# The first expert's left halves gathered straight from x2, weight loads that wait for their buffers alone, and another share of the lo parts on VectorE

## The chip, the core and the metric

One core of a Trainium2 chip runs the whole program in one launch. The metric is the device time of an execution in microseconds (us); lower is better. The profile names the engines PE (TensorE, matmuls; PEld is its loading of weights), DVE (VectorE), ACT (ScalarE), POOL (GpSimd) and SP (SyncE, which issues most DMAs).

## The reference, cut to what matters

Three stages follow each other: attention, a product of matrices for each token, and eight experts that choose their tokens greedily.

```python
attn = softmax(pool2(q) @ k.T / 8) @ v           # 4 x 8 heads, 576 pooled rows, head size 64
x    = attn as [2304, 512]                       # 2304 tokens
x2   = ((x @ w1) * (x @ w2)) @ w3 @ w_out        # w1, w2: 512 x 1024; w3: 1024 x 1024; w_out: 1024 x 512
logits = x2 @ w_gate                             # 2304 x 8
for idx in argsort(-logits.flatten()):           # best pair (token, expert) first
    tok, e = idx // 8, idx % 8
    if assigned[tok] < 0 and counts[e] < 288:
        assigned[tok] = e; counts[e] += 1
for e in range(8):                               # 288 tokens each
    out[mask] = relu(x2[mask] @ e1[e]) @ e2[e]   # 512 -> 1024 -> 512
```

All is in float32. An expert can be computed as soon as its 288 tokens are known, and an expert is full once its last token is found; so the lists come one after the other.

## The kernel before

Every matmul of the later stages multiplies float32 numbers that are split into a high and a low part of a shorter format, in three terms: high x high, low x high and high x low. A high part is a copy made by ACT (`x2h`, `uh`, `exh`, `ehh`); the low part is the number minus its high part, made by DVE or POOL (`x2l`, `ul`, `exl`, `ehl`).

After attention (to about 510 us) and the two products that give h (to about 770 us), three stages follow on PE:

- W = w3 @ w_out, from weights that SP loads back (`w<-w3t`) as buffers come free.
- x2 = h @ W, 18 tiles t of 128 tokens, each 24 matmuls of 512 columns in `pb`. The last three tiles (LATE) are done in two halves of 256 columns, all left halves ahead of the right ones. ACT copies the result to `x2o`, and SP stores it to DRAM: the rows in x2 (shown as `x` in the profile), and the left half of every row once more in x2a.
- the experts, in the order in which their lists come. An expert's rows are gathered by POOL through indirect DMAs (`g<-x,idx`), transposed on PE (`ident,g`), split into `exh` and `exl`, and multiplied: 96 matmuls of 128x288 with the first weights (`exh/exl` with `uh/ul`) and 96 with the second (`ehh/ehl` with `uh/ul`). Eight experts are 1,536 matmuls. The results are transposed back and scattered by POOL.

Only the first expert has its gather in two: the left halves from x2a with its list `idx` into `early`, and the right halves from x2 read as half rows, with `idx_right` = 2 idx + 1. Left halves are there earlier than right ones, so its first six accumulations (AHEAD) begin with the left half of the rows.

Beside W, x2 and the experts a search runs for the next full expert, in seven phases of about 40 to 54 us. It is a loop of round trips: DVE makes masks (`rt_mask`), PE counts with them (`rt_oh,rt_mask`), DVE works on the counts (`rt_cnt`, `rt_own`), PE sums again (`rt_own,rc_ones`), and so on. A phase ends when DVE makes `rt_rows`; from it follow the expert's number (`rows`, which SP reads into a register by a TENSOR_LOAD to address that expert's weights), and its list: `sl_rows`, `sl_oh`, 18 matmuls `sl_mv,sl_oh`, then `idx`.

An expert's weights come in eight pieces ("units") of 128x1024, loaded by SP into a ring of three raw buffers (`u`), whose high part ACT makes and whose low part POOL makes for the first six experts (n < BESIDE = 6), POOL or DVE for the last two. Thirteen such units have room; the first four are kept as halves of 512 columns. Units beyond the fourth wait in three ways: for a raw buffer, for the end of x2 (`gate_main`), and, from HELD = 4 on, for the gathers of the first expert to be issued.

The order of each engine is fixed before the program runs, by a list scheduler that knows a cost for each operation and takes, at each engine, the waiting operation with the lowest priority number. Engines execute strictly in that order. Lines L1501 to L1530 store x2, L1555 to L1586 load and split the units, L1619 ff. gather, L1655 ff. compute an expert.

Of the kernel before, what the change touches and what calls it, by code (L numbers as in the profile page):

```python
# [11 lines left out]
F32 = mybir.dt.float32  # L12
# [1156 lines left out]
def moe_and_experts(tc, sch, env, w1, w2, w3, w_out, w_gate, e1, e2, out):  # L1169
# [330 lines left out]
    def x2_part(t, h, n, xs, xo, pr):  # L1500

        (xh, kxh), (xl, kxl) = xs
        xo, kxo = xo
        cols = slice(h * n, h * n + n)
        ps = Hold(sB)
        for k in range(KF):
            for i, (a, b) in enumerate(((xh, Wh), (xh, Wl), (xl, Wh))):
                def fn(a=a, b=b, k=k, i=i):
                    nc.tensor.matmul(ps.tile[:, :n], a[:, k, :], b[:, k, cols], start=(k == 0 and i == 0), stop=(k == KF - 1 and i == 2))
                acc_op("PE", c_mm(n), fn, [(kxh, k // 4), (kxl, k // 4)] + whole * (t > 1) + [("Wh", k), ("Wl", k)], ps, k == i == 0, pr)  # L1510
        sch.op("ACT", c_act(n), lambda: evac("ACT", xo[:, cols], ps.tile[:, :n]), uses=[ps], w=[(kxo, h)], prio=pr)
        (b, s_), (b1, s1) = divmod(2 * t, NS), divmod(2 * t + 1, NS)

        for dst, w, width, key in ((x2a, DM // 2, DM // 2, "x2a"), (x2, DM, n, "x2")):
            if key == "x2a" and h:
                continue

            for rows, at in ((slice(0, 64), b * SP + s_), (slice(64, 128), b1 * SP + s1)):
                def fn(dst=dst, w=w, width=width, rows=rows, at=at):
                    nc.sync.dma_start(dram(dst, at * w + h * n, [[NS * w, 64], [1, width]]), xo[rows, h * n:h * n + width])  # L1520
                sch.op("DMA", 500, fn, r=[(kxo, h)], w=[(key, t, h)], prio=pr, lat=2300)

    def x2_split(t, pr, lo_e):
# [33 lines left out]
    def unit(w, n, k, pr):  # L1557
# [3 lines left out]
        count[0] += 1  # L1561
        sch.gate = [] if first else gate_main
        raw, free = tt.next([128, 1024], F32, f"u{c}", ("ur", c))
        o = sch.op("DMA", 600, lambda: nc.sync.dma_start(raw[:, :], w[bass.ds(first_row[n][0] + 128 * k, 128), :]), r=[("row", n)],
                   w=[("ur", c)] + free, prio=pr, lat=2800)
        tt.first(o)
        unit_loads.append(o)
        halves = (0, 1) if i < n_pre else (None,)

        lo_e = ("DVE", "POOL") if n >= BESIDE else ("POOL",)  # L1570
        if us[i] is None:
# [45 lines left out]
    def gather(e, pr):  # L1617
# [11 lines left out]
        for h in range(2 if e == 0 else 1):  # L1629
            for j in range(3):  # L1630
                if e == 0:
                    (i2, ki2), keys = (idx2, "idx2") if h else (idx[0], ("idx", 0)), [gs[h][j][1]]
                    dst, src = gs[h][j][0], x2[:, :].rearrange("n (h d) -> (n h) d", h=2) if h else x2a[:, :]
                else:
                    i2, ki2, keys, dst, src = idx[e], ("idx", e), [gs[x][j][1] for x in range(2)], lambda g=rows[j]: g, x2[:, :]

                def fn(j=j, i2=i2, dst=dst, src=src):
                    nc.gpsimd.indirect_dma_start(out=dst(), out_offset=None, in_=src,
                                                 in_offset=bass.IndirectOffsetOnAxis(ap=i2[:, j:j + 1], axis=0))
                sch.gate = [] if e == 0 and h == 0 else gate_main  # L1640
                gathers.append(sch.op("POOL", 1000, fn, r=[ki2] + (x2rows[0] if e == h == 0 else x2rows[1]), w=keys, prio=pr, lat=2500))
        sch.gate = gate_main
# [122 lines left out]
def attention_moe_experts_kernel(ctx, tc, q, k, v, w1, w2, w3, w_out, w_gate, e1, e2, out):  # L1765
# [10 lines left out]
    for r in regions.values():  # L1776
# [40 lines left out]
```

## Time and profile before

| | us |
|---|---|
| median of 3 runs (lowest, highest) | 1228.44 (1225.3, 1230.96) |
| profiled execution, its own time | 1225.08 |
| its span | 1223.3 |
| PE busy / PEld / DVE / ACT / POOL | 1161.6 / 1095.7 / 971.8 / 655.9 / 658.9 |

The span is the time between the first and the last instruction of the profiled execution; its own time is a little longer. The profile numbers each expression by its line; nearly all work of the later stages goes through one helper and has L113, so rows are told apart by their tiles. In a row `out<-in` names what is written and read, and a number in brackets is the time the engine sat idle before it and what ended that. PEclk is the TensorE clock that was granted, 1.00 being full speed.

### The profile page before, as it was taken

The page shows a single profiled execution, that of the slowest core. Times are in us where ns is not written, and L with a number is a line of the kernel's source. Part 1 is how long each engine was busy: PE and PEld are TensorE (multiplying, and loading weights), DVE is VectorE, ACT ScalarE, POOL GpSimd, SP SyncE. Part 2 cuts the span into 40 slices and gives each one's busy share as a digit, 9 for nine tenths or more (in the row PEclk, how much of TensorE's full clock was granted, in tenths as well). Part 3 has the DMA queues.
Part 4 walks back from the last instruction along what each step waited for, and adds up shares of the span by engine and source line. Part 5 has one row for each costly group of instructions (what it writes and reads, how often), then busy time and mean ns, then how long its engine had stood idle before and what let it go on. Part 6 is the DMA issues. An engine that isn't in the chain of part 4 may idle for free.

```text
span 1223.3 us, 24304 instructions
## 1 busy us (share of the span) xinstructions
PE 1161.6 (95%) x8377; PEld 1095.7 (90%) x8377; DVE 971.8 (79%) x2902; ACT 655.9 (54%) x1365; POOL 658.9 (54%) x672
## 2 busy tenths in 40 slices
PE   6999999999999999999999999999998979889996
PEld 5999999999999999889999999777768969889996
DVE  7998999999999999997877787676677687785541
ACT  6887888888888888542222220223222445345530
POOL 4565666666666655554333244236444777679320
PEclk9999999999999999999999999999998989899998
DMA  9676666666666653135555533443224444446620
GB/s 212 153 167 153 152 152 152 152 152 152 151 150 153 151 114 93 41 106 179 168 189 179 173 104 104 145 157 76 59 64 125 158 165 153 142 150 209 201 78 23
DMA packets 116619, 169.89 MB, mean 139 GB/s; under 512 B 47959, under 2 KB 79710, under 8 KB 116494
## 3 DMA queue, kind: packets, MB, share of 16 engines
q1 hardware_dynamic: 113326, 158.89, 48.3%
q0 software_dynamic: 3168, 9.44, 2.5%
q8 instruction: 66, 1.08, 0.4%
q14 instruction: 59, 0.48, 0.1%
HBM read 104.87 MB, written 24.45 MB: 106 GB/s over the span
## 4 chain that ended last, share of the span: by engine, by line
PE 78%; DVE 15%; issue 2%; POOL 1%; DMA 1%; ACT 1%; SPq 0%; DVEq 0%; POOLq 0%; ACTq 0%
PE pb L113 37%; PE s L590 12%; PE pt L614 7%; PE pt L113 6%; PE pt L664 6%; PE s L664 5%; DVE pt L113 4%; PE s L614 3%; DVE cv_v L113 2%; DVE sl_oh L113 1%; PE pt L543 1%; DVE p L600 1%; DVE idx L113 1%; DMA z<-y 1%; DMA vr<-in_v_dram 1%
## 5 line engine op out<-in xcount | busy, mean ns | idle before, releaser
L600 DVE TENSOR_SCALAR_CACHE_REDUCE p<-s 128x384 f32<-128x384 f32 x432 | 230.2, 551 | 34.0 <-PE pt L614 12.5
L590 PE MATMUL s<-kst,qst 128*128 128x384 f32 x768 | 199.7, 359 | 6.3 <-DVE p L600 4.0
L605 ACT ACTIVATE p<-p,mn 128x1152 f32<-128x1152 f32 x144 | 181.1, 1258 | 23.6 <-DVE mn L603 21.4
L113 PE MATMUL pb<-xhi,wh 128*128 128x288 f32 x512 | 156.8, 306 | 1.7 <-ACT wh L113 1.7
L113 PE MATMUL pb<-xlo,wh 128*128 128x288 f32 x512 | 152.5, 298 | 1.9 <-DVE xlo L113 1.7
L113 PE MATMUL pb<-xhi,wl 128*128 128x288 f32 x512 | 152.2, 297 | 1.1 <-DVE wl L113 1.1
L113 POOL TENSOR_TENSOR ul<-u,uh 128x512 fp32r<-128x512 f32 (+1 forms) x68 | 123.9, 1844 | 40.3 <-ACT uh L113 40.0
L590 PEld LDWEIGHTS s<-kst,qst 128*128 128x128 f32 x768 | 123.2, 190 | 12.6 <-DVE p L600 8.8
L614 PE MATMUL pt<-ident,p 128*128 128x128 f32 x879 | 132.8, 273 | 0.3 <-ACT p L605 0.3
L648 DVE TENSOR_TENSOR p_lo<-pt,p_hi 128x384 fp32r<-128x384 f32 x230 | 124.6, 551 | 0.6 <-ACT p_hi L331 0.6
L331 ACT ACTIVATE p_hi<-pt 128x384 fp32r<-128x384 f32 x230 | 106.6, 492 | 12.1 <-PE pt L614 11.7
L614 PEld LDWEIGHTS pt<-ident,p 128*128 128x128 f32 x879 | 107.4, 141 | 4.4 <-ACT p L605 0.5
L113 DVE SCALAR_TENSOR_TENSOR cv_v<-cv_raw,cv_v 128x512 int32<-128x512 int32 (+1 forms) x120 | 102.2, 856 | 6.6 <-POOL cv_raw L113 4.4
L113 PEld LDWEIGHTS pb<-xlo,wh 128*128 128x128 f32 x512 | 97.5, 190 | 2.7 <-DVE xlo L113 2.7
L113 PEld LDWEIGHTS pb<-xhi,wh 128*128 128x128 f32 x512 | 97.4, 190 | 2.5 <-ACT wh L113 1.9
L113 PEld LDWEIGHTS pb<-xhi,wl 128*128 128x128 f32 x512 | 97.3, 190 | 1.3 <-DVE wl L113 1.3
L341 POOL TENSOR_TENSOR p_lo<-praw,p_hi 128x384 fp32r<-128x384 f32 x96 | 97.0, 1018 | 0.4
L113 ACT ACTIVATE a<-pb 128x288 f32<-128x288 f32 x64 | 26.3, 411 | 132.2 <-PE pb L113 126.0
L335 POOL CAST p_hi<-praw 128x384 fp32r<-128x384 f32 x96 | 47.6, 506 | 82.2 <-ACT praw L331 82.1
L113 POOL TENSOR_TENSOR cv_raw<-cv_raw 128x512 f32<-128x512 f32 x40 | 43.2, 1080 | 86.5 <-DVE cv_v L113 67.3
L113 PE MATMUL pb<-ehh,uh 128*128 128x288 f32 x256 | 80.1, 313 | 0.0
L113 PE MATMUL pb<-exh,uh 128*128 128x288 f32 x248 | 78.9, 318 | 0.1
(315 smaller groups left out, 3285.5 us busy)
## 6 DMA issues: line engine op xcount, KB each, us to landing
u<-in_moe_w_dram SPq DMA_DIRECT2D x64, 512.0 KB
cv_raw<-in_moe_w_dram SPq DMA_DIRECT2D x32, 512.0 KB
vr<-in_v_dram SPq DMA_DIRECT2D x32, 288.0 KB
kr<-in_k_dram SPq DMA_DIRECT2D x32, 288.0 KB
kst<-kH SPq DMA_DIRECT2D x31, 288.0 KB
kst<-kL SPq DMA_DIRECT2D x31, 288.0 KB
qr<-in_q_dram SPq DMA_DIRECT2D x15, 576.0 KB
w3t<-wg SPq DMA_DIRECT2D x16, 512.0 KB
```

What stands on the lines that cost most here:

```text
L113: return f(*[x.get() if isinstance(x, Lazy) else x for x in a], **{n: x.get() if isinstance(x, Lazy) else x for n, x in k.items()})
L331: nc.scalar.activation(out, in_, AF.Copy)
L335: nc.gpsimd.tensor_copy(out, in_)
L341: (nc.vector if eng == "DVE" else nc.gpsimd).tensor_tensor(out, a, b, op=OP.subtract)
L543: nc.tensor.transpose(ps.tile[:, a * 128:(a + 1) * 128], r[:, 3 * c + a, :, :].rearrange("p h d -> p (h d)"), ident)
L590: nc.tensor.matmul(ps.tile[:, :384], a[:, :], b[:, cs], start=(n == 0), stop=(n == len(passes) - 1))
L600: sch.op("DVE", c_dve(384), lambda ps=ps, c=c, cs=cs: nc.vector.tensor_scalar(t[:, cs], ps.tile[:, :384], 1.0, BIG, op0=OP.mult, op1=OP.mi ...
L605: sch.op("ACT", c_act(S, psum=False, acc=True), lambda: nc.scalar.activation(t, t, AF.Exp, bias=mn[:, 3:4], scale=-1.0, accum_out=sm[0][:, ...
L614: nc.tensor.transpose(ps.tile[:, a * 128:(a + 1) * 128], t[:, b * 128:(b + 1) * 128], ident)
L648: sch.op("DVE", c_dve(384), lambda view=view, src=src: nc.vector.tensor_tensor(view(lo), src(), view(hi).bitcast(F32), op=OP.subtract), us ...
L664: nc.tensor.matmul(ps.tile[:, :n], vt[:, t, :, :], src[half][:, t, off:off + n], start=(half == 0 and t == 0), stop=(half == 1 and t == NT ...
```

## The change

Three things change.

- x2a and its 36 stores are gone. The first expert's left halves are gathered from x2 read as half rows, with a new list `idx_left` = 2 idx, one more DVE operation. As left gathers and stores of right halves now touch the same array, they are declared independent (`apart`). Six stores from `L16` (64x256) into the right halves of the last three tiles' rows are put at the start of the W stage; the real ones overwrite them.
- A unit's load waits for its raw buffer alone: not for the end of x2, nor for gathers. Its splits still wait as before.
- Low parts of the units of the experts 1, 2, 7 and 8 (n < FILLED = 2 or n >= 6) are made by DVE, those of the experts 3 to 6 by POOL.

```diff
@@ -1491,7 +1491,13 @@
-    x2, x2a = env["x2"], env["x2a"]
+    x2 = env["x2"]
+    halves = {"gathers": [], "stores": []}
+
+    def apart(kind, o):
+        for p in halves["stores" if kind == "gathers" else "gathers"]:
+            tc.declare_no_dep(o.ins, p.ins, reason="the other halves of rows")
+        halves[kind].append(o)
...
@@ -1511,14 +1517,13 @@
-        for dst, w, width, key in ((x2a, DM // 2, DM // 2, "x2a"), (x2, DM, n, "x2")):
-            if key == "x2a" and h:
-                continue
-
-            for rows, at in ((slice(0, 64), b * SP + s_), (slice(64, 128), b1 * SP + s1)):
-                def fn(dst=dst, w=w, width=width, rows=rows, at=at):
-                    nc.sync.dma_start(dram(dst, at * w + h * n, [[NS * w, 64], [1, width]]), xo[rows, h * n:h * n + width])
-                sch.op("DMA", 500, fn, r=[(kxo, h)], w=[(key, t, h)], prio=pr, lat=2300)
+
+        for rows, at in ((slice(0, 64), b * SP + s_), (slice(64, 128), b1 * SP + s1)):
+            def fn(rows=rows, at=at):
+                o = nc.sync.dma_start(dram(x2, at * DM + h * n, [[NS * DM, 64], [1, n]]), xo[rows, h * n:h * n + n])
+                if h:
+                    apart("stores", o)
+            sch.op("DMA", 600, fn, r=[(kxo, h)], w=[("x2", t, h)], prio=pr, lat=2300)
@@ -1530,6 +1535,12 @@
+    for t in range(LAST, N // 128):
+        for x in range(2):
+            b, s_ = divmod(2 * t + x, NS)
+            sch.op("DMA", 600, lambda b=b, s_=s_: nc.sync.dma_start(dram(x2, (b * SP + s_) * DM + DM // 2, [[NS * DM, 64], [1, DM // 2]]),
+                   L16[0:64].rearrange("p c e -> p (c e)")[:, 0:DM // 2]), r=["L16"], w=[("x2", t, 1)], prio=P_W, lat=2300)
@@ -1559,15 +1570,15 @@
-        sch.gate = [] if first else gate_main
+        sch.gate = []
...
         tt.first(o)
-        unit_loads.append(o)
+        sch.gate = [] if first else gate_main
         halves = (0, 1) if i < n_pre else (None,)
-        lo_e = ("DVE", "POOL") if n >= BESIDE else ("POOL",)
+        lo_e = ("POOL",) if FILLED <= n < BESIDE else ("DVE",)
@@ -1594,9 +1605,9 @@
-    x2rows = [[("x2a", t, 0) for t in range(N // 128)], [("x2", t, h) for t in range(N // 128) for h in range(1 + (t >= LAST))]]
+    x2rows = [[("x2", t, 0) for t in range(N // 128)], [("x2", t, h) for t in range(N // 128) for h in range(1 + (t >= LAST))]]
@@ -1629,16 +1640,18 @@
-                    (i2, ki2), keys = (idx2, "idx2") if h else (idx[0], ("idx", 0)), [gs[h][j][1]]
-                    dst, src = gs[h][j][0], x2[:, :].rearrange("n (h d) -> (n h) d", h=2) if h else x2a[:, :]
+                    (i2, ki2), keys = ((idx2, "idx2"), (idx1, "idx1"))[1 - h], [gs[h][j][1]]
+                    dst, src = gs[h][j][0], x2[:, :].rearrange("n (h d) -> (n h) d", h=2)
...
+                    if e == h == 0:
+                        apart("gathers", o)
@@ -1719,14 +1732,14 @@
+    idx1 = rreg.tile([96, 3], I32, name="idx_left")
...
+    sch.op("DVE", 70, lambda: nc.vector.tensor_scalar(idx1, idx[0], 2.0, None, op0=OP.mult), r=[("idx", 0)], w=["idx1"], prio=P_L)
...
-    for o in unit_loads[HELD:]:
-        o.sdeps.update(gathers)
@@ -1754,7 +1767,7 @@
-HELD = 4
+FILLED = 2
```

The scheduler then orders all engines anew. Three places show it. `x_216` in the rows on SP is x2, and numbers behind a name tell its copies apart.

On PE, at the end of x2 and the start of the first expert, before (the list's matmuls `sl_mv,sl_oh`, then the transposes of the left halves, `early`):

```order
L113 LDWEIGHTS sl_oh_9626
L113 MATMUL pt_67<-sl_mv_10056,sl_oh_9626 96x6
L113 MATMUL pt_65<-ident,early 128x96 x3
L113 MATMUL pt_66<-ident,early 128x96 x3
L113 LDWEIGHTS rt_mask_9273
L113 MATMUL pt_67<-rt_oh_9230,rt_mask_9273 90x48
...
L113 MATMUL pb_6498<-exh_10952,uh_0_9669 128x288
L113 MATMUL pb_6498<-exl_10958,uh_0_9669 128x288
L113 MATMUL pb_6498<-exh_10952,ul_0_9689 128x288
```

On PE at the same place in the changed kernel, from the last routing matmuls beside x2 on (`rc_ones` and `rc_tris` are constants):

```order
L113 LDWEIGHTS rt_mask_9215
L113 MATMUL pt_65<-rt_oh_9232,rt_mask_9215 90x48
L113 LDWEIGHTS rc_ones_145
L113 MATMUL pt_67<-rt_own_9188,rc_ones_145 128x120
L113 LDWEIGHTS rc_tris
L113 MATMUL pt_66<-sl_rows_10046,rc_tris 128x1
L113 MATMUL pt_65<-ident,early 128x96 x3
L113 MATMUL pt_67<-ident,early 128x96 x3
L113 MATMUL pb_6497<-exh_10905,uh_0_9674 128x288
L113 MATMUL pb_6497<-exl_10908,uh_0_9674 128x288
L113 MATMUL pb_6497<-exh_10905,ul_0_9680 128x288
```

The transposes of the left halves now stand directly behind the matmul of `sl_rows`, and the first expert's matmuls ahead of the list's; before they stood behind the list.

On DVE, in the fourth phase of the search, beside the first expert, before:

```order
L113 TENSOR_TENSOR rt_mask_9273<-pt_68,rt_thr_9269 128x270
L113 TENSOR_TENSOR exl_10958<-pt_66,exh_10952 128x288 x2
L113 TENSOR_TENSOR rt_cnt_9286<-pt_66,rc_diag 90x48
L113 TENSOR_REDUCE pt_68<-rt_cnt_9286 90x8
L113 TENSOR_TENSOR rt_own_9188<-pt_68,rc_thr 90x120
L113 SCALAR_TENSOR_TENSOR ehl_11097<-pb_6498,ehh_11089 128x288
L113 SCALAR_TENSOR_TENSOR ehl_11106<-pb_6526,ehh_11095 128x288
L113 SCALAR_TENSOR_TENSOR ehl_11116<-pb_6520,ehh_11102 128x288
L113 TENSOR_REDUCE pt_68<-pt_66 128x15
L113 SCALAR_TENSOR_TENSOR ehl_11124<-pb_6478,ehh_11114 128x288
```

On DVE at the same place in the changed kernel (`u` and `uh` are a unit's raw buffer and its high part):

```order
L113 TENSOR_TENSOR rt_mask_9215<-pt_68,rt_thr_9312 128x270
L113 TENSOR_TENSOR ul_11019<-u_10970,uh_11007 128x1024
L113 TENSOR_TENSOR exl_10908<-pt_65,exh_10905 128x288
L113 TENSOR_TENSOR ul_11028<-u_10987,uh_11021 128x1024
L113 TENSOR_TENSOR ul_11041<-u_11003,uh_11026 128x1024
L113 TENSOR_TENSOR exl_10908<-pt_65,exh_10905 128x288
L113 TENSOR_TENSOR rt_cnt_9245<-pt_65,rc_diag 90x48
L113 TENSOR_REDUCE pt_68<-rt_cnt_9245 90x8
L113 TENSOR_TENSOR rt_own_9188<-pt_68,rc_thr 90x120
L113 TENSOR_TENSOR ul_11084<-u_11024,uh_11068 128x1024
L113 TENSOR_REDUCE pt_68<-pt_65 128x15
L113 SCALAR_TENSOR_TENSOR ehl_11104<-pb_6497,ehh_11082 128x288
```

Low parts of units (`ul`, 1024 columns) now stand between the steps of the search. In the whole phase there are nine of 1024 and six of 512 columns; before there were none.

On SP, at the end of x2's stores, before (`rows` is the third expert's number, `u` the load of the next unit):

```order
L113 DMA x_216<-x2o_9803 64x256
L113 DMA x2a<-x2o_9865 64x256
L113 DMA x_216<-x2o_9865 64x256 x2
L113 DMA x_216<-x2o_9803 64x256
L1606 TENSOR_LOAD rows_10866
L113 DMA x_216<-x2o_9865 64x256
L113 DMA x_216<-x2o_9739 64x256 x2
L113 ISA
L113 DMA u_10997<-in_moe_w_dram 128x1024
```

On SP at the same place in the changed kernel:

```order
L113 DMA x_216<-x2o_9861 64x256
L113 DMA x_216<-x2o_9806 64x256
L113 DMA x_216<-x2o_9744 64x256
L113 DMA x_216<-x2o_9861 64x256
L1617 TENSOR_LOAD rows_10860
L113 DMA x_216<-x2o_9744 64x256
L113 ISA
L113 DMA u_10970<-in_moe_w_dram 128x1024
```

The last store now stands behind the load of the number, where three did before, and no store to x2a is left.

Counted in the order of PE, this many of the experts' 1,536 matmuls stand ahead of these points:

| point in the search | before | now |
|---|---|---|
| matmuls of the third list | 0 | 18 |
| rows that end phase 4 | 192 | 267 |
| rows that end phase 5 | 453 | 543 |
| rows that end phase 6 | 720 | 786 |
| the last list | 807 | 897 |

On DVE eight low parts of 512 columns stand in the first phase, where there were none. In the fourth phase there are now 8 exl and 13 ehl instead of 3 and 8, and the two `x2l` that stood in it come ahead of it; in the fifth there are 19 exl and ehl instead of 20, in the sixth 12 instead of 16. On POOL the fourth phase has 4 low parts of 1024 and 2 of 512 columns instead of 9 and 3.

## Rows read from the trace of the kernel before

**Rows 1.** The page's chain that ended last, by engine.

```profile
PE 78%; DVE 15%; issue 2%; POOL 1%; DMA 1%; ACT 1%; SPq 0%; DVEq 0%; POOLq 0%; ACTq 0%
```

**Rows 2.** Windows: length, busy us (count) of PE, PEld, DVE, ACT, POOL; PEclk, DMA, GB/s.

```profile
809.10:849.70 40.60, 38.35 (x202) 28.80 (x202) 30.16 (x122) 14.24 (x25) 24.27 (x23) 1.00 0.37 104
849.70:889.80 40.10, 38.11 (x202) 28.69 (x202) 29.10 (x121) 10.51 (x19) 17.66 (x17) 1.00 0.28 64
889.80:930.20 40.40, 37.89 (x242) 30.92 (x242) 29.66 (x122) 10.42 (x19) 16.21 (x16) 1.00 0.26 60
930.20:980.00 49.80, 43.54 (x326) 41.03 (x324) 34.58 (x135) 18.13 (x32) 32.91 (x23) 0.90 0.50 157
980.00:1034.00 54.00, 46.73 (x357) 45.08 (x357) 41.40 (x141) 26.82 (x50) 41.10 (x37) 0.91 0.48 160
1034.00:1084.40 50.40, 44.75 (x348) 43.17 (x347) 39.09 (x137) 20.68 (x39) 37.79 (x32) 0.93 0.48 158
1084.40:1105.50 21.10, 17.16 (x155) 16.64 (x155) 19.32 (x66) 10.02 (x21) 14.45 (x21) 1.00 0.40 130
1105.50:1213.50 108.00, 105.45 (x811) 104.72 (x810) 47.97 (x70) 43.15 (x82) 42.33 (x40) 1.00 0.42 133
```

**Rows 3.** TensorE's longest waits, 939 to 1106: total us, times, longest.

```profile
PE pt L113 <- DVE exl L113: 8.4, 4, 2.8
PE pt L113 <- DVE rt_mask L113: 4.0, 2, 3.6
```

**Rows 4.** TensorE's groups, 1105.5 to 1213.5: count, busy, mean, idle before.

```profile
L113 PE MATMUL pb<-ehh,uh 128*128 128x288 f32 x128 | 38.3, 299 | 0.0
L113 PE MATMUL pb<-exl,uh 128*128 128x288 f32 x115 | 34.0, 296 | 0.0
```

**Rows 5.** Timeline of VectorE: start, duration, operation, idle before.

```profile
1142.53 0.69 DVE L113 TENSOR_TENSOR ul<-u,uh 128x512 fp32r<-128x512 f32 x1 [1.38 <-ACT uh L113]
1162.43 1.23 DVE L113 TENSOR_TENSOR ul<-u,uh 128x1024 fp32r<-128x1024 f32 x1 [1.00 <-ACT uh L113]
```

**Rows 6.** Timeline of SyncE, GpSimd and TensorE, 929 to 945.

```profile
929.41 1.09 SPq L113 DMA_DIRECT2D x2a<-x2o  x2
...
932.90 0.59 SPq L113 DMA_DIRECT2D x2a<-x2o  x1
933.53 7.32 SPq L113 DMA_DIRECT2D x<-x2o  x6
935.95 1.61 POOL L113 DMA_INDIRECT early<-x2a,idx  x1 [2.54 <-DMA x<-x2o]
941.91 1.38 PE L113 MATMUL pt<-sl_mv,sl_oh 128*96 128x6 bf16 x12 [2.50 <-DVE sl_oh L113]
943.30 0.95 POOL L113 DMA_INDIRECT g<-x,idx_right  x1 [1.97 <-DMA x<-x2o]
```

**Rows 7.** Timeline of SyncE, loads of the W stage.

```profile
773.65 25.06 SPq L113 DMA_DIRECT2D w<-w3t  x9
```

**Rows 8.** VectorE's and GpSimd's groups by form, 820 to 1213.

```profile
L113 DVE SCALAR_TENSOR_TENSOR ehl<-pb,ehh 128x288 fp32r<-128x288 f32 x62 | 27.5, 451 | 17.9 <-ACT ehh L113 14.1 <-issue 2.6 <-ACT uh L113 0.7
L113 DVE TENSOR_TENSOR x2l<-hraw,x2h 128x512 fp32r<-128x512 f32 x2 | 1.4, 684 | 0.0
L113 POOL TENSOR_TENSOR ul<-u,uh 128x1024 fp32r<-128x1024 f32 x34 | 80.9, 2399 | 33.4 <-ACT uh L113 33.1
```

**Rows 9.** VectorE's waits, 930.2 to 980.

```profile
DVE rt_cnt L113 <- PE pt L113: 4.4, 5, 1.4
DVE pt L113 <- PE pt L113: 3.8, 4, 1.0
```

**Rows 10.** Timeline of VectorE and GpSimd around two idx operations.

```profile
944.58 0.17 DVE L113 SCALAR_TENSOR_TENSOR idx<-sl_fl 96x3 int32<-96x3 f32 x1
1047.77 7.31 POOL L113 TENSOR_TENSOR ul<-u,uh 128x512 fp32r<-128x512 f32 x5
1051.27 3.84 DVE L113 SCALAR_TENSOR_TENSOR idx<-sl_fl 96x3 int32<-96x3 f32 x1
```

More of the change, by code (lines that the diff above doesn't have):

```diff
@@ L1596, in moe_and_experts @@
     r_y, r_o = ring(P3, "ey", 4, [128, CAP], F32), ring(P3, "eo", 3, [96, DM], F32)
-    scat, unit_loads, gathers = [], [], []
+    scat = []
     spacer = G.tile([1, 1], F32, name="spacer")
-    x2rows = [[("x2a", t, 0) for t in range(N // 128)], [("x2", t, h) for t in range(N // 128) for h in range(1 + (t >= LAST))]]
+    x2rows = [[("x2", t, 0) for t in range(N // 128)], [("x2", t, h) for t in range(N // 128) for h in range(1 + (t >= LAST))]]
     first_row = [[] for _ in range(8)]
@@ L1631, in gather, with fn @@
                 if e == 0:
-                    (i2, ki2), keys = (idx2, "idx2") if h else (idx[0], ("idx", 0)), [gs[h][j][1]]
-                    dst, src = gs[h][j][0], x2[:, :].rearrange("n (h d) -> (n h) d", h=2) if h else x2a[:, :]
+                    (i2, ki2), keys = ((idx2, "idx2"), (idx1, "idx1"))[1 - h], [gs[h][j][1]]
+                    dst, src = gs[h][j][0], x2[:, :].rearrange("n (h d) -> (n h) d", h=2)
                 else:
                     i2, ki2, keys, dst, src = idx[e], ("idx", e), [gs[x][j][1] for x in range(2)], lambda g=rows[j]: g, x2[:, :]
-                def fn(j=j, i2=i2, dst=dst, src=src):
-                    nc.gpsimd.indirect_dma_start(out=dst(), out_offset=None, in_=src,
-                                                 in_offset=bass.IndirectOffsetOnAxis(ap=i2[:, j:j + 1], axis=0))
+                def fn(j=j, h=h, i2=i2, dst=dst, src=src):
+                    o = nc.gpsimd.indirect_dma_start(out=dst(), out_offset=None, in_=src,
+                                                     in_offset=bass.IndirectOffsetOnAxis(ap=i2[:, j:j + 1], axis=0))
+                    if e == h == 0:
+                        apart("gathers", o)
                 sch.gate = [] if e == 0 and h == 0 else gate_main
-                gathers.append(sch.op("POOL", 1000, fn, r=[ki2] + (x2rows[0] if e == h == 0 else x2rows[1]), w=keys, prio=pr, lat=2500))
+                sch.op("POOL", 1000, fn, r=[ki2] + (x2rows[0] if e == h == 0 else x2rows[1]), w=keys, prio=pr, lat=2500)
         sch.gate = gate_main
@@ L1786, in attention_moe_experts_kernel @@
     env = {"nc": nc, "G": G, "xT": xT, "main": regions["main"], "prep": regions["prep"], "psS": regions["psS"],
-           "s_pt": s_pt, "pts": pts, "ident": ident, "rc": rc, "xreg": regions["x"], "x2": dpool.tile([N, DM], F32, name="x2"), "x2a": dpool.tile([N, DM // 2], F32, name="x2a"), "w3t": dpool.tile([8, 128, 2, 1024], F32, name="w3t"),
+           "s_pt": s_pt, "pts": pts, "ident": ident, "rc": rc, "xreg": regions["x"], "x2": dpool.tile([N, DM], F32, name="x2"), "w3t": dpool.tile([8, 128, 2, 1024], F32, name="w3t"),
            "wof": dpool.tile([8, 128, 2, DM], F32, name="wof")}
```

## The prediction

> **What bounds the kernel now.** The chain that ended last is three quarters TensorE [rows 1], so I cut the part after the W stage into stretches at the points where routing has found its rows, the mark where one expert's search ends and the next begins [rows 2]. In the first three stretches (beside x2) TensorE is busy for 38 of 40 us and VectorE for 29 to 30, so TensorE sets the pace and VectorE has about 10 us free in each. In the next three TensorE is busy for 43.54 of 49.80, 46.73 of 54.00 and 44.75 of 50.40 us, and in the fourth, up to the last list's matmuls, for 17.16 of 21.10: 6.26 + 7.27 + 5.65 + 3.94 = 23.1 us without work, and its granted clock in the first three is 0.90 to 0.93 of full. The waits behind that name VectorE, above all the exl parts and the routing masks [rows 3]. In the last stretch TensorE is busy for 105.45 of 108.00 us: nothing but its own work bounds it.
>
> So the end is the time at which the last list is known, plus the expert matmuls that still stand behind it on TensorE. After the last list 729 of the 1,536 (3 x 128 + 3 x 115) run in 108.0 us [rows 2, 4]: 108.0 / 729 = 0.148 us each, transposes included. A change helps by making the last list earlier or by putting matmuls ahead of it. This one does the second at the price of the first: counted in TensorE's order, 897 expert matmuls stand before the last list instead of 807, so 639 stay behind it, 90 fewer.
>
> **The change, part by part**, as shifts of the end.
>
> *Matmuls behind the last list.* 90 x 0.148 = -13.3 us. This holds only if TensorE does them in time it now loses, since its whole work is unchanged: they must fit into the 23.1 us above.
>
> *The search of phases 1 to 3 gets later.* Eight lo parts of 512 columns go from GpSimd to VectorE in phase 1: 8 x 0.69 = 5.5 us by the one at 1142.53 [rows 5]. VectorE has about 10 us free in that stretch, but in pieces between round trips, and the parts stand in its order where the search stands too. TensorE's order says the same: the routing rows that end phase 1 come after the equivalent of 126 x2 matmuls of 512 columns instead of 112, those that end phase 3 after 420.5 instead of 403.5. In a stretch of 40.1 to 40.4 us some 146 of these pass, 0.275 us each with all that lies between, so 14 are 3.9 us and 17 are 4.7. I take +4; the bounds are 0 (all eight in the gaps) and +5.5 (none). x2 itself does not end later, as TensorE has other work in its order meanwhile.
>
> *Left halves gathered from x2.* The 36 stores into the copy cost SP about 0.55 us each to issue (two in 1.09 us), and the last of them, at 932.90, stands behind x2's own stores; the first early gather goes out at 935.95 [rows 6]. With the left halves stored once, the last one can leave SP some 2 to 3 us sooner, and the gather near 933. I cost this at nothing: in the new order the transposes of `early` stand on TensorE behind the matmuls of rt_own and sl_rows, which come with the search, about 4 us later than now. Before, they stood behind the list matmuls (941.91 on, held by VectorE [rows 6]). So the first expert matmul may come up to 1 us earlier or later, within TensorE's idle time there, and the search does not hang on it. The additional operation for idx_left, on 96 x 3 numbers, is nothing beside a stretch of 40 us.
>
> *The last right halves.* The last store of a right half now stands on SP behind the load of the third expert's row number, which VectorE writes at the end of phase 3. Now six x2 stores go out from 933.53 for 7.32 us, the last at about 940.5, and the right gathers follow at 943.30 [rows 6]; behind a row number that comes 4 us later, they go out 1 to 2 us later. The matmuls that need them stand after 18 left ones and the list; 0, bound +2.
>
> *Dummy stores.* Six of them, 6 x 0.55 = 3.3 us of SP, stand among the loads of the W stage. Nine of these loads go out in 25.06 us, 2.8 us apart, as buffers come free [rows 7]: SP has time to spare between them, and only the first, at 773.65, has two stores ahead of it with nothing before. So 0, bound +1 (two issues, if that piece lands late).
>
> *Phase 4 on VectorE.* It has 34.58 us of work in 49.80 [rows 2]. Two x2l parts leave it (2 x 0.68 [rows 8]). In come nine lo parts of 1024 columns at 1.23 and six of 512 at 0.69 (9 x 1.23 + 6 x 0.69 = 15.2) [rows 5], and five exl and five ehl parts at 0.45 (4.5) [rows 8]. That is 34.6 - 1.4 + 15.2 + 4.5 = 52.9 us (exl, on the same 128 x 288 numbers, taken at the price of ehl). The 15.2 us of idle time in the phase are mostly waits for TensorE's routing results (4.4 and 3.8 us [rows 9]) and for exh; work that stands ready fills a part of them. I keep 5 of the 15: 58 us, +8.2. The lower bound is TensorE's: 75 more expert matmuls before the fifth search are 75 x 0.148 = 11.1 us, 43.5 + 11.1 = 54.6, so +4.8 even if VectorE loses nothing. The upper bound is all 15.2 us kept: 68.1, +18.3.
>
> *Phases 5 and 6, and up to the last list.* VectorE does one and four exl or ehl fewer: -0.45 and -1.8, so -2.25. GpSimd has 4 + 2 lo parts in phase 4 instead of 9 + 3, and about as many as before later; I take nothing for its weaker hold on VectorE.
>
> Where VectorE and GpSimd meet: the operation that makes idx takes 0.17 us in a quiet place (944.58), and 3.84 us at 1051.27, where it ended together with five lo parts on GpSimd that ran from 1047.77 for 7.31 us [rows 10]. So a two-operand operation of VectorE waited there for more than one part of GpSimd (these five took 1.46 us each, and a part of 1024 columns takes 2.40 [rows 8]). The Trainium skill, page "SBUF — State Buffer", section "Who interferes with whom", says that a VectorE instruction with two SBUF inputs and a GpSimd instruction that reads SBUF exclude each other, for the whole of the instruction that issued first. By that rule alone a wait would end with one GpSimd instruction; the row shows a wait over several, so here the measurement goes further than the rule, and the new lo parts on VectorE, all with two such inputs, are what it speaks against.
>
> *Sum.* Last list: +4 + 8.2 - 2.25 = +10.0. End: +10.0 - 13.3 = -3.3. The profiled execution took 1225.08 us, with a span of 1223.3, so its own forecast is 1221.8. The median shown, 1228.44, is 3.4 above it; against the median I forecast 1228.4 - 3.3 = 1225.1.
>
> **Rivals.**
>
> A. Faster: VectorE's new work goes into its gaps. Phase 4 is then bound by TensorE (+4.8), phases 1 to 3 cost 0, phases 5 and 6 give -2.25, and one of the waits like that of idx [rows 10] goes with GpSimd's shorter runs (-3.7). The last list moves by -1.1, the end by -14.4: 1214. For it: VectorE is idle for 10 us in each of the three x2 stretches and 15.2 in phase 4, and TensorE's granted clock of 0.90 to 0.93 there leaves room upwards. Against it: those gaps are answers that VectorE waits for, each about 1 us, and a lo part of 1.23 us put into one is longer than the gap.
>
> B. Slower: the gaps of phase 4 do not fill. Place: the round trips of phase 4. VectorE sends a mask and waits for TensorE, on which 75 more expert matmuls now stand between the rounds; the lo parts then add to the phase in full. Price: +18.3 instead of +8.2, last list +20.1, end +6.8: 1235.2; with the late start at its bound of 5.5 and the -2.25 gone, 1239. From a phase 4 of 61.4 us on no gain is left; slower by over 0.5% begins at 67.5. For it: VectorE executes in order, a lo part whose hi part is late on ScalarE holds the search, and ScalarE's hi parts now stand between the exh. Against it: nearly all of the phase's idle time would have to survive while VectorE's work rises by half.
>
> C. The lo parts on VectorE wait for GpSimd's runs, as idx does. GpSimd is busy for 32.91 us in phase 4 [rows 2]; without five parts of 1024 columns and one of 512 (about 13.3) it is 19.6 of 58, a third, so 5 of the 15 meet one, at half of the 3.67 us by which idx was late: 5 x 1.8 = 9. The end moves by -3.3 + 9 = +5.7: 1234.1. For it: [rows 10]. Against it: GpSimd's own runs of lo parts in phase 4 are halved.
>
> D. The change does not do what its first part says, as the early gather is not what the first matmuls wait for. That is in the forecast already, as nothing.
>
> **Chances.** The forecast 0.46 (its own range 1218 to 1231), A 0.24, B 0.20, C 0.10. A change within 0.5% (6.1 us, 1222.3 to 1234.6) is about what cannot be told from none here. Of the forecast's 0.46, 0.16 lie below 1222.3, 0.28 within and 0.02 above; of A, 0.22 below and 0.02 within; of B, 0.17 above and 0.03 within; of C, 0.05 and 0.05. So faster 0.38, same 0.38, slower 0.24. The range 1212 to 1238 takes in A at 1214, C, and B at its price of 1235; it leaves out B at both bounds and an A in which more than one such wait of VectorE goes.
>
> **What would show it.** In the profile after: phase 4, between the third and the fourth mark of routing rows, takes 58 us with VectorE busy for 53; the last list is ready about 10 us later against the end of the W stage; from it to the end of TensorE's work 639 matmuls take 95 us; early gathers near 933 with their transposes at 942 to 943, held by sl_rows. Wrong would be: a phase 4 of 55 us or less (A) or 65 or more (B), lo parts on VectorE with a mean far above 1.23 us (C), a first expert matmul before 941, or a W stage longer by some us (the dummy stores).

## The result, and the profile after

The changed kernel takes 1217.14 us (median of 5 runs, 1215.0 to 1218.63), the kernel before 1227.6 (5 runs, 1225.3 to 1230.96). The ratio is 0.9907, 95% interval 0.9888 to 0.9926: 10.5 us faster, where 3.3 were forecast. The profiled execution took 1218.05 us with a span of 1216.1. TensorE's first matmul of the W stage starts 1.8 us later in it (770.74 against 768.92), with nothing changed ahead; so the stages are compared by their own lengths.

The windows of the changed kernel between the same marks, in the columns of [rows 2]:

```profile
810.90:855.30 44.40, 41.33 (x217) 31.32 (x215) 34.34 (x132) 15.30 (x27) 15.55 (x15) 1.00 0.40 123
855.30:895.40 40.10, 38.14 (x203) 28.69 (x201) 29.11 (x122) 10.67 (x19) 17.34 (x17) 1.00 0.18 40
895.40:936.70 41.30, 38.64 (x260) 32.46 (x259) 31.58 (x124) 10.84 (x20) 15.65 (x16) 1.00 0.19 44
936.70:998.00 61.30, 51.82 (x385) 49.34 (x384) 49.12 (x158) 29.16 (x51) 31.05 (x30) 0.89 0.57 181
998.00:1045.30 47.30, 45.75 (x367) 44.20 (x366) 36.72 (x140) 22.93 (x44) 38.14 (x31) 0.96 0.50 170
1045.30:1092.50 47.20, 42.18 (x337) 40.52 (x336) 36.49 (x134) 21.27 (x40) 32.17 (x30) 0.96 0.43 141
1092.50:1114.20 21.70, 19.96 (x168) 19.50 (x167) 19.92 (x72) 9.60 (x18) 16.40 (x18) 0.92 0.45 149
1114.20:1206.40 92.20, 92.07 (x708) 91.83 (x708) 38.04 (x65) 34.20 (x67) 15.81 (x25) 1.00 0.36 113
```

Against [rows 2] the stretches change by +3.8, 0, +0.9, +11.5, -6.7, -3.2, +0.6 and -15.8 us: -8.9 together. The search is 6.9 us later at its end, and 15.8 us less is left behind the last list. Phase 4 is 3.3 us longer than forecast, and phases 5 and 6 give most of its growth back.

The waits of the changed kernel in phase 4, four of VectorE's and one of ScalarE's (us in total, times, longest):

```profile
DVE ehl L113 <- ACT ehh L113: 3.6, 5, 1.2
DVE rt_cnt L113 <- PE pt L113: 2.6, 4, 1.0
DVE pt L113 <- PE pt L113: 2.1, 3, 1.0
DVE ul L113 <- ACT uh L113: 1.3, 3, 0.5
ACT uh L113 <- DMA u<-in_moe_w_dram: 13.9, 8, 7.0
```

and VectorE's lo parts there, by form (busy, mean ns, idle before):

```profile
L113 DVE TENSOR_TENSOR ul<-u,uh 128x1024 fp32r<-128x1024 f32 x9 | 10.9, 1216 | 0.7 <-ACT uh L113 0.7
L113 DVE TENSOR_TENSOR ul<-u,uh 128x512 fp32r<-128x512 f32 x6 | 4.1, 684 | 0.5 <-ACT uh L113 0.5
```

The 15 lo parts took the durations that the prediction used (10.9 + 4.1 = 15.0 us); none waited for GpSimd. But VectorE's idle time shrank only from 15.2 to 61.30 - 49.12 = 12.2 us, not to 5.

The timeline of the changed kernel at the start of the first expert, rows of GpSimd, TensorE, VectorE and SyncE (start, duration, idle time before):

```profile
936.01 1.38 POOL L113 DMA_INDIRECT early<-x,idx_left  x1 [8.96 <-issue]
...
942.34 0.27 PE L113 MATMUL pt<-rt_oh,rt_mask 128*90 128x48 bf16 x3 [1.98 <-DVE rt_oh L113]
944.64 0.26 PE L113 MATMUL pt<-rt_own,rc_ones 97*128 97x120 f16 x1 [2.03 <-DVE rt_own L113]
...
947.39 0.95 POOL L113 DMA_INDIRECT g<-x,idx_right  x1 [0.23 <-issue]
950.52 1.21 DVE L113 TENSOR_TENSOR ul<-u,uh 128x1024 fp32r<-128x1024 f32 x1
951.86 7.78 SPq L113 DMA_DIRECT2D u<-in_moe_w_dram  x4
...
959.70 0.74 PE L113 MATMUL pt<-ident,g 96*128 96x96 f32 x3 [2.61 <-DVE exl L113]
```

The early gather goes out at 936.01, before at 935.95 [rows 6]; counted from the start of the W stage that is 1.8 us sooner. TensorE then waits for the search: for rt_oh (1.98 us) and rt_own (2.03), as the new order puts `early` behind both. The eighth unit is loaded only at 951.86, once the lo part of the fifth, which VectorE makes at 950.52 among the steps of the search, has freed a raw buffer; ScalarE waits 13.9 us in the phase for such loads.

Two operations of the search with two inputs in SBUF, the scan that opens a phase and idx, in the kernel before from phase 5 on (one more, 1051.27, stands in [rows 10]):

```profile
980.02 2.95 DVE L113 TENSOR_TENSOR_SCAN pt<-rc_rst,rt_ge 128x144 f32<-128x144 f32 x1
999.72 3.88 DVE L113 SCALAR_TENSOR_TENSOR idx<-sl_fl 96x3 int32<-96x3 f32 x1
1034.02 1.95 DVE L113 TENSOR_TENSOR_SCAN pt<-rc_rst,rt_ge 128x144 f32<-128x144 f32 x1
1084.40 2.75 DVE L113 TENSOR_TENSOR_SCAN pt<-rc_rst,rt_ge 128x144 f32<-128x144 f32 x1
```

and in the changed one (its two other scans took 0.45 and 0.46 us):

```profile
997.92 1.53 DVE L113 TENSOR_TENSOR_SCAN pt<-rc_rst,rt_ge 128x144 f32<-128x144 f32 x1
1016.25 0.39 DVE L113 SCALAR_TENSOR_TENSOR idx<-sl_fl 96x3 int32<-96x3 f32 x1
1060.20 3.75 DVE L113 SCALAR_TENSOR_TENSOR idx<-sl_fl 96x3 int32<-96x3 f32 x1
1109.83 1.31 DVE L113 SCALAR_TENSOR_TENSOR idx<-sl_fl 96x3 int32<-96x3 f32 x1
```

Undisturbed they take 0.46 and 0.16 us. Beyond that the five before lose 13.7 us from phase 5 on, the four after 6.0. That is 7.6 us of the 9.3 by which the search gets shorter from phase 5 to the last list.

### The profile page after: what moved, and what is told of

Its sections match the earlier page's. It is cut to its first block, busy times and chain, and to the rows that moved or that the text cites. A ratio compares the mean times of both kernels' runs of the same rounds, so it can differ in the third digit from the quotient of the medians.

```text
span 1216.1 us, 24258 instructions
## 1 busy us (share of the span) xinstructions
PE 1159.5 (95%) x8377; PEld 1093.1 (90%) x8377; DVE 976.6 (80%) x2930; ACT 655.7 (54%) x1365; POOL 613.9 (50%) x645
## 4 chain that ended last, share of the span: by engine, by line
PE 77%; DVE 15%; DMA 3%; issue 2%; SPq 1%; POOL 1%; ACT 1%; DVEq 0%; POOLq 0%; ACTq 0%
PE pb L113 37%; PE s L590 12%; PE pt L614 7%; PE pt L664 6%; PE pt L113 6%; PE s L664 5%; DVE pt L113 3%; PE s L614 3%; DVE cv_v L113 2%; DMA u<-in_moe_w_dram 1%; DVE p L600 1%; DVE p_lo L648 1%; PE pt L543 1%; DVE sl_oh L113 1%; DMA cv_raw<-in_moe_w_dram 1%
## 5 line engine op out<-in xcount | busy, mean ns | idle before, releaser
L590 PEld LDWEIGHTS s<-kst,qst 128*128 128x128 f32 x768 | 124.3, 192 | 11.4 <-DVE p L600 7.6
L113 POOL TENSOR_TENSOR ul<-u,uh 128x1024 fp32r<-128x1024 f32 (+1 forms) x41 | 77.1, 1904 | 21.8 <-ACT uh L113 21.8
```

Source lines behind the costliest of these rows:

```text
L113: return f(*[x.get() if isinstance(x, Lazy) else x for x in a], **{n: x.get() if isinstance(x, Lazy) else x for n, x in k.items()})
L590: nc.tensor.matmul(ps.tile[:, :384], a[:, :], b[:, cs], start=(n == 0), stop=(n == len(passes) - 1))
```

## The experiments

All twelve at a glance. "Last list" and "tail" are from the profiled execution: from the first matmul of the W stage to the last list's matmuls, and from there to TensorE's end. "Waits" is what the scans, idx and VectorE's lo parts took beyond their undisturbed durations beside GpSimd, up to the last list. Where lo parts of phase 1 stand on VectorE, 0.7 us of it is one of them. A third operation of the search with two inputs in SBUF, the one that makes `rt_pend` anew, is not counted: it lost 0.9 us in e5, 1.1 in e6 and 0.4 in the changed kernel. Ratios are to the kernel before, run beside each on the same chip, where its median was 1228 to 1231 us. e1 to e4 share a chip, e5 to e8 a second and e9 to e12 a third, so across these groups the ratios are compared and not the medians. A profiled execution need not be a typical one: that of e2 took 1218.1 us, that of e10 1207.9.

| kernel | median us | ratio, 95% interval | last list | tail | waits |
|---|---|---|---|---|---|
| before | 1227.6 | 1 | 335.7 | 109.9 | 14.2 |
| changed | 1217.1 | 0.9907 (0.9888 to 0.9926) | 342.5 | 94.1 | 8.1 |
| e1 before, idx from PSUM | 1217.5 | 0.9900 (0.9864 to 0.9937) | 327.6 | 110.6 | 7.8 |
| e2 changed, idx from PSUM | 1212.2 | 0.9847 (0.9811 to 0.9883) | 340.4 | 94.1 | 3.0 |
| e3 lo parts only | 1217.2 | 0.9900 (0.9869 to 0.9932) | 345.1 | 93.7 | 7.5 |
| e4 changed without lo parts | 1212.5 | 0.9870 (0.9835 to 0.9905) | 322.0 | 110.5 | 7.1 |
| e5 left halves only | 1230.1 | 0.9996 (0.9972 to 1.0019) | 341.0 | 109.8 | 17.5 |
| e6 free loads only | 1223.5 | 0.9954 (0.9926 to 0.9981) | 334.5 | 110.3 | 15.2 |
| e7 e4, idx from PSUM | 1210.2 | 0.9838 (0.9800 to 0.9876) | 321.2 | 110.0 | 4.5 |
| e8 e7, scan from PSUM | 1208.6 | 0.9829 (0.9791 to 0.9867) | 320.5 | 109.2 | 0 |
| e9 before, idx and scan from PSUM | 1212.1 | 0.9863 (0.9842 to 0.9884) | 321.3 | 110.4 | 0 |
| e10 changed, idx and scan from PSUM | 1212.0 | 0.9861 (0.9840 to 0.9882) | 335.5 | 94.1 | 0.7 |
| e11 free loads, idx and scan from PSUM | 1208.2 | 0.9837 (0.9811 to 0.9863) | 317.4 | 109.3 | 0 |
| e12 e8, last two experts' lo parts on VectorE | 1207.6 | 0.9828 (0.9803 to 0.9853) | 320.6 | 107.6 | 0 |

**e1 and e2: idx without its second SBUF input.** The order of all engines stays.

```diff
-        dve(3, lambda: nc.vector.scalar_tensor_tensor(idx[n], fl[:, 0], 256.0, fl[:, 1], op0=OP.mult, op1=OP.add),
-            [kf], [("idx", n)])
+        dve(3, lambda: nc.vector.scalar_tensor_tensor(idx[n], ps2.tile[:96, 0:3], 256.0, fl[:, 1], op0=OP.mult, op1=OP.add),
+            [kf], [("idx", n)], uses=[ps2])
```

> The kernel before, where the operation that makes idx reads one of its two inputs from PSUM (the list matmuls' result) and only the other from SBUF; the order on all engines is that of before. Theory L (VectorE's operations with two SBUF inputs wait out whole GpSimd runs, and that is on the path of the search): idx takes 0.2 us instead of 3.88 and 3.84 in phases 5 and 6, the last list comes 7.4 us earlier and the end moves by up to as much, about -7 (1220 to 1222). Rival W (phases 5 and 6 got shorter in the changed kernel only because the second expert's work stands ahead; the wait of idx is slack): no change, 1227 to 1228.

> The changed kernel with the same edit of idx; order unchanged. L: the remaining waits of idx, 3.59 us in phase 6 and 1.15 at the last but one list, go, the last list and the end come 3.6 to 4.7 us earlier: 1212.5 to 1213.5. W: no change, 1217.

Measured: 1217.5, some 3 us more of a gain than L gave, and 1212.2. W falls. This one operand gives the kernel before as much as the whole change. The timeline of e1 (GpSimd, then VectorE; the last row is a scan, which is left as it was):

```profile
999.74 2.38 POOL L113 TENSOR_TENSOR ul<-u,uh 128x1024 fp32r<-128x1024 f32 x1
1000.56 0.15 DVE L113 SCALAR_TENSOR_TENSOR idx<-pt,sl_fl 96x3 int32<-96x3 f32 x1
980.76 2.98 DVE L113 TENSOR_TENSOR_SCAN pt<-rc_rst,rt_ge 128x144 f32<-128x144 f32 x1
```

idx takes 0.15 us in the middle of a lo part on GpSimd, where it took 3.88; the scan still takes 2.98. In e1 the waits fall by 6.4 us and the last list comes 8.1 us earlier, so a wait costs somewhat more than itself.

**e3 and e4: the lo parts alone, and the change without them.**

```diff
-        lo_e = ("DVE", "POOL") if n >= BESIDE else ("POOL",)
+        lo_e = ("POOL",) if FILLED <= n < BESIDE else ("DVE",)
```

(in e3 put into the kernel before; in e4 taken back in the changed one)

> The kernel before with the third part of the change alone (lo parts of experts 1, 2, 7, 8 on VectorE); x2a, its stores and the held loads stay. In TensorE's order 897 expert matmuls stand ahead of the last list, as in the changed kernel. Theory S (the search and the matmuls behind the last list make the end; copy and held loads cost nothing): as the changed kernel, 1216 to 1219. Rival G (the early gather and the free loads give the gain): 1224 to 1228.

> The changed kernel with the lo parts placed as before; x2a stays away and loads are not held. 807 expert matmuls stand ahead of the last list, as in the kernel before. S: as before, 1226 to 1229. G: 1217 to 1221.

e3 came out as S said, 1217.2. e4 did as neither said: 1212.5, by the medians faster than the whole change (the intervals of the two ratios overlap a little). With 807 matmuls ahead of the last list, as before, it has that list 13.7 us earlier than before, and the tail of before. Its timeline, GpSimd and then VectorE:

```profile
994.90 2.39 POOL L113 TENSOR_TENSOR ul<-u,uh 128x1024 fp32r<-128x1024 f32 x1
996.09 1.22 DVE L113 SCALAR_TENSOR_TENSOR idx<-sl_fl 96x3 int32<-96x3 f32 x1
```

and its windows of phases 5 and 6, in the columns of [rows 2]:

```profile
979.80:1026.20 46.40, 43.43 (x355) 41.55 (x354) 37.21 (x140) 22.84 (x42) 38.42 (x34) 1.00 0.50 169
1026.20:1072.30 46.10, 42.21 (x350) 40.58 (x349) 37.16 (x140) 23.30 (x43) 38.67 (x32) 1.00 0.53 176
```

The phases are 7.6 and 4.3 us shorter than [rows 2], at a granted clock of 1.00 instead of 0.91 and 0.93; idx waits 1.06 us beyond its 0.16 instead of 3.7. That idx ends with the lo part that runs (994.90 + 2.39); GpSimd's next one starts only 1.5 us later.

**e5 and e6: the two other parts, each alone in the kernel before.** The edits are the first two parts of the diff above.

> The kernel before with the first part of the change alone: x2a and its stores away, left halves gathered from x2, six dummy stores. Order of TensorE and VectorE as before. Theory F (the gain of the kernel without the lo parts comes from the loads, which let GpSimd start earlier and bring the second expert's rows forward): 1226 to 1229, no change. Rival G (the gather from x2 gives it): 1214 to 1220.

> The kernel before with the second part alone: unit loads wait for raw buffers alone. The second expert's transposes stand behind 174 expert matmuls instead of 192; 798 stand ahead of the last list. F: 1212 to 1217, as without the lo parts; waits of two-input operations in phases 5 and 6 down from 11.4 us to about 5, granted clock 1.00 there. G: 1225 to 1229.

e5: no change, with waits that are 3.3 us longer than before in its profile; G falls. e6: 0.46% faster (5.6 us, interval 2.3 to 9.1), not the 11 to 16 that F said, and the waits in its phases 5 and 6 stayed (12.4 us). So parts 1 and 2 do not add up to e4. The two kernels' last lists are 12.5 us apart, and 8.1 of that are waits, 7.1 us instead of 15.2; without any waits the same two, e11 and e8 below, are equal. With such waits in the way, two nearly equal orders differ by several us.

**e7 to e12: without the waits.** The scan copies its second input to PSUM first, and works there.

```diff
-            dve(288, lambda ge=ge, inc=inc: nc.vector.tensor_tensor_scan(
-                inc.rearrange("p e c -> p (e c)"), c["rst"].rearrange("p e c -> p (e c)"),
-                ge[:, 1].rearrange("p e c -> p (e c)"), 0.0, op0=OP.mult, op1=OP.add), [(kge, 1)], [kin])
+            def f(ge=ge, inc=inc):
+                nc.vector.tensor_copy(inc, ge[:, 1])
+                nc.vector.tensor_tensor_scan(inc.rearrange("p e c -> p (e c)"), c["rst"].rearrange("p e c -> p (e c)"),
+                                             inc.rearrange("p e c -> p (e c)"), 0.0, op0=OP.mult, op1=OP.add)
+            dve(288, f, [(kge, 1)], [kin])
```

> The changed kernel with the lo parts placed as before and idx made from PSUM and SBUF. Theory L: the waits of idx in phases 5 and 6 (1.06 and 1.54 us) go: 2.6 us off 1212.5, 1209 to 1211. Rival: the next operation with two SBUF inputs waits instead, 1212 to 1213.

> As the last one, and the scan at the start of each phase reads its second input from PSUM, after a copy there (about 0.3 us more per phase). L: its waits (0.99 + 1.22 + 1.76 us) go, less 3 x 0.3: another 3 us, 1206 to 1208. Rival: no change or slower by the copies, 1210 to 1213.

1210.2, as L gave, and 1208.6, 0.6 above it; each step alone is within the noise, and no wait of this kind is left in e8.

> The kernel before with idx and the phase's scan each reading one input from PSUM (the scan after a copy there): of the search's operations with long waits none has two SBUF inputs any more. 807 expert matmuls ahead of the last list. L one for one: 14.2 us of waits go, 7 copies of 0.3 come, last list 12 us earlier, 1216 to 1218; with more coming after each wait, as idx alone showed (8.1 us for 6.4), 1211 to 1215.

> The changed kernel with the same two edits. Theory M (the prediction's sum of -3.3 holds and missed only the waits behind GpSimd): about 3 us faster than the kernel before with the same edits. Rival N (the lo parts cost more than the 90 matmuls give, and the change gains by moving VectorE out of GpSimd's way alone): not faster than the kernel before with the same edits, by 0 to 4 us slower; 1210 to 1213.

e9: 1212.1, as L gave with more coming after each wait; two operands moved to PSUM take 1.4% off the kernel before. Its timeline, GpSimd and then VectorE, and its windows of phases 5 and 6 in the columns of [rows 2]:

```profile
979.24 1.26 POOL L113 TENSOR_TENSOR ul<-u,uh 128x512 fp32r<-128x512 f32 x1
979.43 0.46 DVE L113 TENSOR_TENSOR_SCAN pt<-rc_rst,pt 128x144 f32<-128x144 f32 x1
996.68 0.15 DVE L113 SCALAR_TENSOR_TENSOR idx<-pt,sl_fl 96x3 int32<-96x3 f32 x1
...
979.43:1025.70 46.27, 43.34 (x356) 41.72 (x357) 35.59 (x142) 25.71 (x48) 40.61 (x36) 1.00 0.54 185
1025.70:1069.75 44.05, 42.16 (x350) 40.94 (x349) 34.28 (x137) 21.23 (x39) 38.14 (x33) 1.00 0.54 182
```

The scan now takes 0.46 us beside a lo part on GpSimd. The two phases are 14.1 us shorter than in [rows 2], for 11.4 us of waits that went, and the granted clock is 1.00 instead of 0.91 and 0.93. TensorE's busy time in them falls by 6.0 us for as many operations, so a part of the gain may come with the clock; no run separates that part.

e10: 1212.0, no difference to e9 (the two ratios' intervals allow some 3.6 us either way; in the profiled executions the last list is 14.2 us later and the tail 16.3 shorter, -2.1). So without the waits the change gains at most some 4 us and may lose as much; M and N can't be told apart by this. A gain near 10 is ruled out.

> The second part alone (loads not held) with the same two edits. If free loads help by the second expert's rows, which come forward: 2 to 5 us faster than the kernel before with the two edits. If only by the waits behind GpSimd: the same as that.

e11: 1208.2, 3.9 us below e9, and its last list comes 3.9 us earlier in the profile: without any waits the free loads are worth about 4 us, with an interval as large. e8, with parts 1 and 2, has a ratio of 0.9829; e10, with part 3 beside them, 0.9861: 3.9 us, less than the some 5 us that the two intervals allow. That the lo parts on VectorE cost something once nothing waits for GpSimd is likely, and not shown.

The last edit, against e8:

```diff
-        lo_e = ("DVE", "POOL") if n >= BESIDE else ("POOL",)
+        lo_e = ("DVE",) if n >= BESIDE else ("POOL",)
```

> The fastest version so far (parts 1 and 2, idx and scan from PSUM) with the lo parts of the last two experts on VectorE alone: order to the last list unchanged. If GpSimd's lo parts hold TensorE in the tail (108 us for 729 matmuls before, 92.2 for 639 after): 1206 to 1208. Rival: no change, 1208.6.

e12: 1207.6, the lowest median, but by the ratio equal to e8 (0.9828 and 0.9829), so the gain is not shown; its tail is 1.6 us shorter in the profile. Like e8 it beats both kernels: 1.7% (21 us) under the kernel before, some 10 us under the changed one.

## Why the prediction was right in direction and range, and wrong in size

The direction and the range 1212 to 1238 held. But 1217.1 lies just outside the forecast's own 1218 to 1231 and nearer to rival A's price of 1214, while A's mechanism did not come: phase 4 grew by 11.5 us and not 4.8. Rival B put the end of any gain at a phase 4 of 61.4 us; it took 61.3, and the gain came all the same. That the range held is in part luck: two terms came out dearer, and waits that went, for which the forecast had nothing, outweighed them.

*Matmuls behind the last list: -13.3.* Mechanism right, mis-sized by 2.5: -15.8 between the windows. 92.2 / 639 is 0.144 us each instead of 0.148; before, TensorE was idle for 108.00 - 105.45 = 2.55 us of that stretch, 2.4 of it in one wait for exl (the first row; the other two are GpSimd and VectorE there):

```profile
PE pt L113 <- DVE exl L113: 2.4, 1, 2.4
...
1104.84 6.13 POOL L113 TENSOR_TENSOR ul<-u,uh 128x512 fp32r<-128x512 f32 x4
1105.76 5.23 DVE L113 SCALAR_TENSOR_TENSOR idx<-sl_fl 96x3 int32<-96x3 f32 x1
```

After, it is idle for 0.13. The longest wait of idx in the kernel before is the last one, 5.23 us at 1105.76, behind the last list's matmuls; it is not in the table and costs nothing that shows: without it, in e1 and e9, the tail is as long (110.6 and 110.4 us for 109.9).

*Phases 1 to 3: +4.* Right: +3.8 + 0 + 0.9 = +4.7, nearly all in phase 1, where the eight lo parts stand.

*Left halves, right halves, dummy stores: 0.* Right as a sum: e5, which has all three alone, shows no change. The early gather came 1.8 us sooner against the W stage, where I had put it 3 us sooner.

*Phase 4: +8.2.* Mis-sized: +11.5, in the pair without waits +10.8 (50.0 and 60.8 us). VectorE's busy time was over-estimated (49.1 for 52.9) and the idle time that survives under-estimated (12.2 for 5).

The prediction added up whole durations. By the timeline these rose by 17.4 us for the 18.3 forecast (nine exl and ehl came, not ten). But operations of VectorE overlap their neighbours by some 0.1 us in the timeline, and the time in which it is busy rose by 14.5 alone. The lo part of 952.15 begins before the operation of 952.03 has ended (the last two rows are waits of the kernel before in phase 4):

```profile
952.03 0.20 DVE L113 TENSOR_TENSOR rt_cnt<-pt,rc_diag 90x48 f16<-90x48 f32 x1 [0.30 <-PE pt L113]
952.15 1.21 DVE L113 TENSOR_TENSOR ul<-u,uh 128x1024 fp32r<-128x1024 f32 x1
...
DVE exl L113 <- ACT exh L113: 2.0, 2, 1.3
DVE ehl L113 <- ACT ehh L113: 0.5, 1, 0.5
```

For the idle time, the step that failed is the choice of 5 behind "work that stands ready fills a part of them". Some was filled: VectorE's waits for TensorE's counts fell from 8.2 us [rows 9] to 4.7 (2.6 and 2.1). But its waits for ScalarE's high parts grew from 2.5 us to 4.9 (3.6 and 1.3), as each lo part, exl and ehl needs one; that is what rival B had for it. The phase's growth lies between the forecast and rival B (+18.3), nearer the forecast.

*Phases 5 and 6: -2.25.* This term was mis-sized most, by its sentence "I take nothing for its weaker hold on VectorE". They and the piece behind them changed by -9.3 us, and 7.6 us of that are waits behind GpSimd that went. Rival A had put one such wait (-3.7) into its price. That one went (999.72, now 0.39), one stayed (3.75), a new one of 1.31 came, and the three scans fell from 7.65 us together to 2.44. e9 and e10 show that the gain beyond the forecast hangs on these waits: with them taken from both kernels, no difference is left that can be measured.

*Free loads.* The prediction has no term for the second part at all. e6 and e11 price it at 4 to 6 us when the lo parts stay on GpSimd. In the changed kernel parts 1 and 2 show nothing: e3, without them, is as fast (0.9900 and 0.9907).

The deviations add up: -3.3 forecast, +0.7 in phases 1 to 3, +3.3 in phase 4, -7.0 from phase 5 to the last list, -2.5 in the tail: -8.8, against -8.9 between the two profiles. Rival C, lo parts on VectorE that wait for GpSimd, did not come in phase 4: their means were 1.216 us and 0.684. It was not put to the test there either, as GpSimd's lo parts began after the last of VectorE's (the first two rows). Where the two meet, one waits; the last two rows are from the tail of the kernel before, where such a part takes VectorE 1.22 us alone:

```profile
982.16 0.68 DVE L113 TENSOR_TENSOR ul<-u,uh 128x512 fp32r<-128x512 f32 x1
983.49 7.26 POOL L113 TENSOR_TENSOR ul<-u,uh 128x512 fp32r<-128x512 f32 x4 [6.03 <-ACT uh L113]
...
1157.51 2.47 POOL L113 TENSOR_TENSOR ul<-u,uh 128x1024 fp32r<-128x1024 f32 x1 [9.33 <-ACT uh L113]
1158.40 2.67 DVE L113 TENSOR_TENSOR ul<-u,uh 128x1024 fp32r<-128x1024 f32 x1 [0.68 <-ACT uh L113]
```

On those waits the prediction's reading needs two corrections. The five lo parts of [rows 10] are four of 512 columns and one of 1024, as a merged row names the shape of its first instruction, so 1.46 us is a mean over two shapes; the idx of 1051.27 waited for three of the five. And a wait can end before the run does. The lo parts on GpSimd around the idx of 999.72 in the kernel before, one by one:

```profile
998.89 2.38 POOL L113 TENSOR_TENSOR ul<-u,uh 128x1024 fp32r<-128x1024 f32 x1
1001.24 2.34 POOL L113 TENSOR_TENSOR ul<-u,uh 128x1024 fp32r<-128x1024 f32 x1
1003.55 2.34 POOL L113 TENSOR_TENSOR ul<-u,uh 128x1024 fp32r<-128x1024 f32 x1
```

idx ended at 1003.60, as the third of them began, not at the end of the run: it had waited for the rest of one and for the whole of the next. The Trainium skill, "SBUF — State Buffer", section "Who interferes with whom", has such a pair exclude each other for the whole of the instruction that issued first. The trace agrees where idx ended with the part that ran (e4, 1.22 us), and differs where it let one or more pass. That section also says that an operation with at most one SBUF input, outside VectorE's two-port modes, does not contend; e1 and e9 agree (0.15 and 0.46 us beside a running lo part).

One operation with a single input in SBUF did wait, off the search's path; no row tells its mode. In the kernel before it took 1.10 us, up to the end of a lo part on GpSimd that began at 822.63; in the changed kernel, where none runs then, 0.15:

```profile
822.86 1.10 DVE L113 TENSOR_SCALAR idx_right<-idx 96x3 int32<-96x3 int32 x1
```

Over the timelines of all fourteen kernels I count 52 waits of scans, idx and rt_pend of over 0.2 us. Each ends at a fixed distance behind the end of a GpSimd instruction (idx and rt_pend some 0.03 us, the scan 0.33), in 46 of them one that no other followed directly. So what sets most waits is how many GpSimd instructions stand back to back from there on. The five waits of the scans and idx from the start of phase 5 to the start of phase 7 take, with the one that runs, 1, 1, 2, 1 and 2 lo parts in e4, and 3, 3, 2, 3 and 2 in e5, where the longest is (GpSimd, then VectorE):

```profile
998.04 8.24 POOL L113 TENSOR_TENSOR ul<-u,uh 128x512 fp32r<-128x512 f32 x4
1000.12 6.18 DVE L113 SCALAR_TENSOR_TENSOR idx<-sl_fl 96x3 int32<-96x3 f32 x1
```

What stays open: why in 6 of the 52 VectorE came in between two GpSimd instructions that follow each other directly, as at 1003.60, and in the others did not.

## What to carry to other kernels

Before work is moved between VectorE and GpSimd, list the small operations on the critical engine that take many times their usual duration, and look at what GpSimd does just then; giving each of two such operations one operand from PSUM took 1.4% off this kernel, with the order as it was but for one copy a phase. When two parts of a change share such a resource, their effects do not add up (e3, e4, e5 and e6), so take the shared wait away first, and then price each part. And each part of a diff needs its own term in the sum, also the one that only lets loads go earlier.

## What the runs showed of the hardware that had not been expected

A 96 x 3 operation on VectorE, 0.16 us by itself, took 3.88 and 3.84 us beside elementwise work on GpSimd, and 6.18 in e5, past the end of the GpSimd instruction that ran when it came; with one of two inputs in PSUM it took 0.15 us beside the same work. Such a wait is no idle time in the profile: the waiting operation itself is shown longer.
